# Attention of the first two tiles on diagonal quadrants, with the weight loads cut finer and reordered

## The chip, the cores and the metric

The kernel runs on one core of a Trainium2 chip. The core has a matrix engine, TensorE (PE in the profile; PEld is its loading of weights), a vector engine (DVE), a scalar engine (ACT) for copies and functions such as exp and Gelu, GpSimd (POOL), and SyncE (SP), whose queue issues the DMAs here. SBUF is the working memory, 128 partitions wide; matrix products land in PSUM, which has eight banks of 128 x 512 float32. The metric is the time of one execution on the device, in microseconds.

## What is computed

Attention in chunks of 64 keys, then a two-layer network with an exact Gelu on its result:

```python
q_c = q.reshape(B, H, nc, chunk, D)          # 8, 8, 9, 64, 64; k_c, v_c likewise
scores = scale * np.matmul(q_c, k_c.transpose(0, 1, 2, 4, 3))
attn = softmax(scores)                       # along the last axis
x = np.matmul(attn, v_c)                     # per token the 8 heads side by side: 4608 x 512
h = x @ w_in                                 # 512 x 2048
g = 0.5 * h * (1.0 + erf(h / sqrt(2)))
out = g @ w_out                              # 2048 x 512
```

All inputs and the output are float32; the kernel multiplies in bfloat16.

## The kernel before

The 4608 tokens are handled in nine tiles of 512: tile t takes the first eight chunks of batch t, and the ninth tile the last chunk of every batch. Inside a tile the eight heads form four groups `g` of two; the two heads of a group lie on partitions 0 to 63 and 64 to 127. For each tile there is attention (transposes of q and k, scores, exp, sums, the product with v), which leaves `x` in four parts `x[:, ks, :]`, one for each group; then the first matmul (`h`, 16 blocks `f`, each over the four `ks`, followed by Gelu on ACT) and the second (`y`). From tile 1 on parts of both matmuls are done in seven products instead of eight; from tile 2 on the attention uses four 64x64 quadrants of TensorE (`quad_S`, `quad_av`). All of that stays as it is.

The order of all work is written out by hand (`with tc.manual_schedule()`, L1097): each engine does its instructions in the order in which the lines are run. The change touches the stretch up to tile 1.

**Attention of tiles 0 and 1.** `att_units` makes four lists: `T` (two transposes' units for each group, q then k: `att_Tq`, `att_Tk`), `S_` (`att_S`), `U` (the sums and their reciprocals) and `A` (`att_av`). `att_S` and `att_av` multiply one chunk at a time with a 128x128 block-diagonal left operand, so that both heads of a group go through one full-width matmul of 64 columns. For that, `k_bds` (one for each group) and `v_bds` (one for each tile) hold zeros beside the blocks: `zero_k` on POOL and `zero_v` on DVE for tile 0 (L1105 to L1112), two memsets on POOL for tile 1 (L1172). `att_Tk` copies the transposed k from PSUM in two halves of 64 partitions, `cast_v` casts v in four pieces a group. `transposed` takes its bank from `ps_tp`, which has two; only tile 0's k uses `ps_mm`. The scores and products of tile 1's groups 2 and 3 use `ps_tp` as well, everything else of the attention `ps_at` (three banks, of which one holds y rows during tile 0's second matmul).

**Loads.** All go through SP's queue in the order of the program into six staging buffers (`stage_tile`): tile 0's q and k for each group, v, then w_in in four parts of 1 MB (`load_w_in`; part 0 to 2 as two DMAs each), w_out in four parts (`load_w_out`, one DMA each), with tile 1's q after w_out's first part, its k after the second, and its v last. Each weight part is cast to bfloat16 in four pieces by `win[c](i, ...)` and `wout[c](i, ...)`; piece `i` of `win[c]` is block f = 4c + i, and piece `i` of `wout[c]` is row block f = 4c + i of w_out.

**First matmul of tile 0.** `mm1_slices` (L1203) does f = 0 and 1 with `ks` outermost, `mm1_slot` the others one by one. In tile 0 every 512-column matmul is issued as two of 256 by `by_halves` (its rows stand under L465).

**Second matmul of tile 0.** `phase(0, ..., by_rows=True)` runs 16 steps: step f = 0 to 11 is `mm2_rows(0, f)`, four matmuls for one row block of w_out (L1025; for f = 2 to 4 by halves), and steps 12 to 15 are `mm2_slot` (L989), the last quarter of one of the four token blocks, after which that block is copied out. The dictionary in the call says which units of tile 1's attention stand ahead of which step. TensorE works in this order, so a unit that waits holds up the steps behind it.

```python
        phase(0, {0: [lambda: act_table(Act.Exp)],
                      2: [T[0]], 3: [T[2]], 4: [T[4], T[6]], 7: [T[1], T[3]], 8: [T[5], S_[0]],
                      9: [T[7], S_[1], next_qk], 10: [S_[2], lambda: att_sum(1, 0), lambda: wout[3](2, DV)],
```

Tile 1's first matmul begins right behind (`mm1_slices`, L481), with `A[3]` inside it (`last_av`).

Of the kernel before, what the change touches and what calls it, by code (L numbers as in the profile page):

```python
# [11 lines left out]
def kernel(  # L12
# [10 lines left out]
    P = 128  # L23
# [46 lines left out]

    def zero_v(i, eng):
        eng.memset(v_bds[i][0:CH, :, :, CH:P], 0.0)
        eng.memset(v_bds[i][CH:P, :, :, 0:CH], 0.0)

    def zero_k(k_bd, eng):
        eng.memset(k_bd[0:CH, :, CH:P], 0.0)
        eng.memset(k_bd[CH:P, :, 0:CH], 0.0)
# [99 lines left out]
    def load_v(t):  # L177

        tiles[t]["vf"] = stage_tile()[:].rearrange("p (h n d) -> p h n d", h=H, d=D)
        for h in range(H):  # L180
            nc.sync.dma_start(tiles[t]["vf"][:, h], v[t, h, 0:MT, :].rearrange("(n key) d -> key n d", key=P))  # L181
# [16 lines left out]
    def cast_v(t, g, r, copies):  # L198
        to = slice(CH * r, CH * (r + 1))
        for c, copy in enumerate(copies):  # L200
            copy(v_bds[t % NV][to, c:CT:2, g, to], tiles[t]["vf"][CH * c:CH * (c + 1), 2 * g + r])
# [14 lines left out]
    def att_Tk(t, g, copy):  # L216
        tp = transposed(t, "k", g)
        for r in range(2):
            sl = slice(CH * r, CH * (r + 1))
            copy(k_bds[g][sl, :, sl].rearrange("p i (c j) -> p i c j", j=J), tp[sl])  # L220
# [139 lines left out]

    def att_S(t, g):
# [3 lines left out]
        for i in range(CT):  # L365
            nc.tensor.matmul(s_ps[:, i, :], k_bds[g][:, i, :], st["qT", g][:, i], start=True, stop=True)
# [68 lines left out]
    def att_av(t, g):  # L435
# [3 lines left out]
        for i in range(CT):  # L439
            nc.tensor.matmul(av_ps[:, i, :], v_bds[t % NV][:, i, g, :], st["pT", g][:, i, :], start=True, stop=True)  # L440
# [19 lines left out]
    def by_halves(to, left, right, start, stop):  # L460

        n = to.shape[-1] // 2
        for a in range(2):
            cols = slice(n * a, n * (a + 1))
            nc.tensor.matmul(to[:, cols], left, right[:, cols], start=(start and a == 0), stop=stop, skip_group_check=True)  # L465

    def mm1_slices(t, pools, steps):
# [4 lines left out]
        for step in steps:  # L472
# [3 lines left out]
            for ks in step[1]:  # L476
                for f in step[0]:
# [3 lines left out]
                    (nc.tensor.matmul if t else by_halves)(h_ps[f][:], w_in_sb[:, ks, f * P:(f + 1) * P], st["x"][:, ks, :],  # L481
# [615 lines left out]
    with tc.manual_schedule():  # L1097
# [17 lines left out]
        for g in range(G - 1):  # L1115
            for r in range(2):
                cast_v(0, g, r, (PO, PO))
# [67 lines left out]
        for i in range(FC):  # L1185
            wout[2](i, PO)
# [181 lines left out]
```

## Time and profile before

| | us |
|---|---|
| median of 3 runs | 267.13 (266.97 to 267.51) |
| the profiled execution | 267.09 |
| its span | 265.5 |
| granted TensorE clock, share of full | 0.997 |
| first matmul of tile 0 starts | 17.95 |
| second matmul of tile 0 starts | 32.42 |
| tile 1's first matmul starts | 50.97 |

In the timeline a row holds the start in us, the time to the end of its last instruction, the engine, the line, the operation, what it writes and reads, the shapes, and how many instructions it joins; in brackets stands how long the engine was idle before it and what ended that. A matmul row's end includes the way through the array, so costs of TensorE are better taken from one start to the next. In the chain, each row is the piece of work that the next one waited for. In a table of groups, the numbers behind the first bar are the busy time in us and the mean ns of one, behind the second the idle time before them. In a table of windows, the busy time of each engine is followed by the number of its instructions; the last three columns are the granted clock, the busy share of the 16 DMA engines and GB/s. DMA queue rows give packets, MB and the share of 16 engines' time.

### The profile page before, as it was taken

To read this page: it belongs to the slowest core of one execution; us is meant where nothing else is said; L and a number is where in the kernel's file an instruction comes from. 1 tells how busy PE (TensorE), PEld (TensorE's weight loads), DVE (VectorE), ACT (ScalarE), POOL (GpSimd) and SP (SyncE) were. 2 spreads that over 40 slices of the span, in tenths; PEclk is the share of its full clock that TensorE was granted. 3 is DMA by queue.
4 is the path that set the end of the run, shared out by engine and by line. 5 is a ranking of instruction groups with operands and counts; after the bars stand their busy time and mean duration, and the time that the engine had idled before them with its cause. 6 is when DMAs were issued, how large, how long until landed. Compare 5 with 4: busy or idle time off the path is not lost.

```text
span 265.5 us, 7854 instructions
## 1 busy us (share of the span) xinstructions
PE 256.1 (96%) x3122; PEld 210.6 (79%) x3122; DVE 223.1 (84%) x394; ACT 190.5 (72%) x386; POOL 103.2 (39%) x225
## 2 busy tenths in 40 slices
PE   6789999999999999999999999999999999999993
PEld 2478875556888888887888888888888888888882
DVE  6874986898897599678999999999999999948772
ACT  3856758987767987898888588947894789227720
POOL 7767778702364291481372095009411300000000
PEclk9999999999999999999999999999999999999998
DMA  6999998999979979999999988998973410130014
GB/s 201 268 311 396 395 401 236 283 193 289 243 195 284 220 175 244 275 239 249 276 245 232 267 186 237 217 175 195 264 160 80 134 42 2 41 119 3 2 40 125
DMA packets 123416, 54.02 MB, mean 203 GB/s; under 512 B 97776, under 2 KB 120304, under 8 KB 123376
## 3 DMA queue, kind: packets, MB, share of 16 engines
q1 hardware_dynamic: 123072, 53.23, 77.4%
q8 instruction: 25, 0.41, 0.7%
q10 hardware_dynamic: 304, 0.26, 0.3%
q14 instruction: 15, 0.12, 0.1%
HBM read 36.70 MB, written 9.44 MB: 174 GB/s over the span
## 4 chain that ended last, share of the span: by engine, by line
PE 76%; DMA 10%; ACT 7%; SPq 4%; issue 1%; DVE 0%; POOL 0%
PE hs_ps L601 31%; PE y_ps L761 22%; PE y_ps L791 13%; DMA arrival<-in_moe_w_out_dram 8%; ACT h L609 3%; SPq L181 2%; PE h_ps L491 2%; DMA arrival<-in_moe_w_in_dram 2%; PE av_ps L349 2%; PE h_ps L481 2%; ACT pT L272 2%; SPq L142 1%; PE y_ps L1025 1%; PE y_ps L989 1%; PE s_ps L264 1%; ACT L1095 1%
## 5 line engine op out<-in xcount | busy, mean ns | idle before, releaser
L609 ACT ACTIVATE h<-hs_ps 128x512 bf16<-128x512 f32 x87 | 49.6, 609 | 6.5 <-PE hs_ps L601 5.7
L238 POOL CAST v_nat<-arrival 128x256 bf16<-128x256 f32 x56 | 24.9, 473 | 33.5 <-DMA arrival<-in_v_dram 23.1
L601 PEld LDWEIGHTS <-w_in_sb 128*128 128x128 bf16 x348 | 33.9, 98 | 4.7 <-issue 0.2
L194 POOL CAST q_nat<-arrival 128x256 bf16<-128x256 f32 x40 | 16.8, 467 | 50.2 <-DMA arrival<-in_k_dram 25.3
L601 PE MATMUL hs_ps<-x,w_in_sb 128*128 128x256 bf16 x232 | 31.8, 272 | 0.0
L761 PEld LDWEIGHTS <-h 128*128 128x128 bf16 x240 | 23.2, 98 | 2.8
L1095 ACT ACT_TABLE_LOAD x16 | 20.5, 1283 | 1.3 <-PEq L1352 1.0
L190 POOL CAST k_nat<-arrival 128x256 bf16<-128x256 f32 (+1 forms) x44 | 19.1, 476 | 5.3 <-DMA arrival<-in_k_dram 5.3
L721 ACT COPY kept<-y_ps 128x512 f32<-128x512 f32 (+1 forms) x17 | 9.0, 536 | 16.0 <-PE y_ps L761 15.9
L761 PE MATMUL y_ps<-w_out_sb,h 128*128 128x256 bf16 x160 | 18.6, 273 | 0.0
L761 PE MATMUL y_ps<-v_bd,k_bd 128*128 128x256 bf16 x160 | 18.5, 273 | 0.1
L761 PEld LDWEIGHTS <-k_bd 128*128 128x128 bf16 x160 | 15.6, 98 | 2.1 <-issue 0.2
L618 ACT COPY hs_ps<-hs_ps 128x512 f32<-128x512 f32 x29 | 16.2, 583 | 0.6 <-PE hs_ps L601 0.5
L601 PE MATMUL hs_ps<-k_bd,w_in_sb 128*128 128x256 bf16 x116 | 16.6, 272 | 0.0
L493 ACT ACTIVATE h<-h_ps 128x512 bf16<-128x512 f32 x21 | 12.5, 604 | 5.5 <-PE h_ps L465 4.1
L272 ACT ACTIVATE pT<-s_ps 128x512 bf16<-128x512 f32 x28 | 14.4, 599 | 1.8 <-PE s_ps L264 1.8
L791 PEld LDWEIGHTS <-h 128*128 128x128 bf16 x144 | 13.8, 98 | 1.7
L465 PE MATMUL h_ps<-x,w_in_sb 128*128 128x256 bf16 x128 | 14.5, 273 | 0.1
L601 PE MATMUL hs_ps<-k_bd,w_in_more 128*128 128x256 bf16 x96 | 14.2, 273 | 0.0
L601 PEld LDWEIGHTS <-w_in_more 128*128 128x128 bf16 x128 | 12.5, 98 | 2.0 <-issue 0.3
L726 DVE TENSOR_TENSOR kept<-y_ps,kept 128x512 f32<-128x512 f32 (+1 forms) x16 | 10.4, 651 | 4.3 <-PE y_ps L761 2.3
L465 PEld LDWEIGHTS <-w_in_sb 128*128 128x128 bf16 x128 | 12.3, 98 | 2.1 <-DVE w_in_sb L1070 0.7
(175 smaller groups left out, 638.9 us busy)
## 6 DMA issues: line engine op xcount, KB each, us to landing
arrival<-in_v_dram SPq DMA_DIRECT2D x58, 128.0 KB, 3.2
arrival<-in_k_dram SPq DMA_DIRECT2D x28, 256.0 KB, 5.6
arrival<-in_q_dram SPq DMA_DIRECT2D x7, 1024.0 KB, 6.9
out_dram<-kept SPq DMA_DIRECT2D x24, 256.0 KB, 3.2
arrival<-in_moe_w_out_dram SPq DMA_DIRECT2D x4, 1024.0 KB, 12.1
arrival<-in_moe_w_in_dram SPq DMA_DIRECT2D x6, 512.0 KB, 8.5
out_dram<-y_sb SPq DMA_DIRECT2D x8, 256.0 KB, 2.5
arrival<-in_v_dram SPq DMA_DIRECT2D x28, 64.0 KB, 2.7
```

Source lines behind the costliest of these rows:

```text
L190: copy(st[nm][:, q0:q0 + n, g], st[nm + "f"][:, 2 * q0:2 * (q0 + n), g].rearrange("p (q r) d -> p q r d", r=2))
L194: copy(st[nm][:, g, j:j + 2].rearrange("p j r d -> p r j d"), st[nm + "f"][:, 2 * g:2 * g + 2, j:j + 2])
L238: copy(st["v"][:, r::2, n], st["vf"][:, r::2, n])
L272: nc.scalar.activation(pT[:].rearrange("p u (c j) -> p u c j", j=J), tiles[t]["s_ps"][m // 2][m % 2][:].rearrange("p u (j c) -> p u c j", ...
L465: nc.tensor.matmul(to[:, cols], left, right[:, cols], start=(start and a == 0), stop=stop, skip_group_check=True)
L493: nc.scalar.activation(tiles[t]["h"][:, f, :], h_ps[:], Act.Gelu)
L601: nc.tensor.matmul(hs[:, f], left[:, ks, f * P:(f + 1) * P], right[:, ks], start=(fresh and f == 0 and ks == 0), stop=(ks == 1), skip_grou ...
L609: nc.scalar.activation(h[:, n:n + HM, HD * c:HD * (c + 1)], src, Act.Gelu)
L618: "s11": lambda: AC(place_of("b")[:], bank["a"][:]),
L761: nc.tensor.matmul(to, left(f, m), right[:, f], start=(fresh and (split or m == 0) and f == 0), stop=(f == HF - 1), skip_group_check=True)
L791: nc.tensor.matmul(bank[name][:, m], left(f, m), right[:, f], start=(fresh and m == 0 and f == 0), stop=(f == HF - 1), skip_group_check=True)
L1095: nc.scalar.activation(act_scratch[:], rest[:, 0:1], func)
```

## The change

In tiles 0 and 1, k and v are kept without zeros: the transposed k is copied in one piece into the first 512 columns of `k_bds[g]`, v is loaded so that each head's keys lie on its own 64 partitions and is cast without zeros into the first 2048 columns of `v_bds[t]`. `att_S` and `att_av` do sixteen 64x64 matmuls a group instead of eight full-width ones, alternating between the quadrant of partitions 0 to 63 and that of 64 to 127. All fillings with zeros are gone. w_in's first part comes in four DMAs, every part of w_out and tile 1's q and k in two; w_out's third part is issued ahead of tile 1's k. `by_halves` is gone, and so are the interleaved first two blocks of the first matmul; the order of tile 1's attention among the y rows is new.

```diff
     def load_v(t):
-        tiles[t]["vf"] = stage_tile()[:].rearrange("p (h n d) -> p h n d", h=H, d=D)
+        tiles[t]["vf"] = stage_tile()[:].rearrange("p (g i d) -> p g i d", g=G, d=D)
+        tiles[t]["vr"] = v_bds[t][:].rearrange("p a b c -> p (a b c)")[:, 0:G * MT].rearrange("p (g i d) -> p g i d", g=G, d=D)
         for h in range(H):
-            nc.sync.dma_start(tiles[t]["vf"][:, h], v[t, h, 0:MT, :].rearrange("(n key) d -> key n d", key=P))
+            r = h % 2
+            nc.sync.dma_start(tiles[t]["vf"][CH * r:CH * (r + 1), h // 2],
+                              v[t, h, 0:MT, :].rearrange("(i key) d -> key i d", key=CH))
...
-    def cast_v(t, g, r, copies):
-        to = slice(CH * r, CH * (r + 1))
-        for c, copy in enumerate(copies):
-            copy(v_bds[t % NV][to, c:CT:2, g, to], tiles[t]["vf"][CH * c:CH * (c + 1), 2 * g + r])
+    def cast_v(t, g, copy, n=1):
+        w = CT // n
+        for a in range(0, CT, w):
+            copy(tiles[t]["vr"][:, g, a:a + w], tiles[t]["vf"][:, g, a:a + w])
...
     def att_Tk(t, g, copy):
         tp = transposed(t, "k", g)
-        for r in range(2):
-            sl = slice(CH * r, CH * (r + 1))
-            copy(k_bds[g][sl, :, sl].rearrange("p i (c j) -> p i c j", j=J), tp[sl])
+        kT = k_bds[g][:].rearrange("p i c -> p (i c)")[:, 0:MT].rearrange("p (i c) -> p i c", c=CH)
+        copy(kT.rearrange("p i (c j) -> p i c j", j=J), tp)
+        tiles[t]["kT", g] = kT
...
+    def both_halves(to, left, right):
+        for i in range(CT):
+            for r in range(2):
+                sl = slice(CH * r, CH * (r + 1))
+                nc.tensor.matmul(to(i)[sl], left(i)[sl], right(i)[sl], start=(i == 0), stop=True,
+                                 tile_position=(CH * r, CH * r), skip_group_check=True)
...
-        for i in range(CT):
-            nc.tensor.matmul(s_ps[:, i, :], k_bds[g][:, i, :], st["qT", g][:, i], start=True, stop=True)
+        both_halves(lambda i: s_ps[:, i, :], lambda i: st["kT", g][:, i], lambda i: st["qT", g][:, i])
...
-        for i in range(CT):
-            nc.tensor.matmul(av_ps[:, i, :], v_bds[t % NV][:, i, g, :], st["pT", g][:, i, :], start=True, stop=True)
+        both_halves(lambda i: av_ps[:, i, :], lambda i: st["vr"][:, g, i, :], lambda i: st["pT", g][:, i, :])
...
-                    (nc.tensor.matmul if t else by_halves)(h_ps[f][:], w_in_sb[:, ks, f * P:(f + 1) * P], st["x"][:, ks, :],
+                    nc.tensor.matmul(h_ps[f][:], w_in_sb[:, ks, f * P:(f + 1) * P], st["x"][:, ks, :],
...
-            (by_halves if 2 <= f < 5 else nc.tensor.matmul)(
+            nc.tensor.matmul(
...
     def load_w_out(c):
         raw = stage_tile()[:].rearrange("p (f n) -> p f n", f=FC)
-        nc.sync.dma_start(raw, w_out_v[:, c * FC:(c + 1) * FC, :])
+        for f in range(0, FC, 2):
+            nc.sync.dma_start(raw[:, f:f + 2], w_out_v[:, c * FC + f:c * FC + f + 2, :])
...
-        win = [load_w_in(c, 2) for c in range(NWC - 1)]
+        win = [load_w_in(c, 2 if c else 4) for c in range(NWC - 1)]
...
+        T[2 * G - 2] = lambda: att_Tq(0, G - 1, AC)
...
         for g in range(G - 1):
-            for r in range(2):
-                cast_v(0, g, r, (PO, PO))
-        cast_v(0, G - 1, 0, (PO, PO))
-        win[0](0, PO)
+            cast_v(0, g, PO, 2)
+        win[0](1, PO)
...
-        cast_v(0, G - 1, 1, (DV, DV))
+        cast_v(0, G - 1, DV)
         A[2]()
-        win[0](1, AC)
+        win[0](0, DV)
         p3()
         A[3]()
+        def load_halves(nm):
+            for h in (0, G):
+                load_qk(1, nm, h, h + G)
         win.append(load_w_in(NWC - 1))
         wout = [load_w_out(0)]
-        win[0](2, DV)
+        win[0](2, AC)
         win[0](3, PO)
-        load_qk(1, "q")
+        load_halves("q")
         wout.append(load_w_out(1))
         for c in range(1, NWC):
...
-            if c == 1:
-                load_qk(1, "k")
+            if c == 2:
+                load_halves("k")
             else:
-                wout.append(load_w_out(c))
-            if c < 3:
-                r = slice(CH * (c - 1), CH * c)
-                o = slice(CH * (2 - c), CH * (3 - c))
-                nc.gpsimd.memset(v_bds[1][r, :, :, o], 0.0)
+                wout.append(load_w_out(2 if c == 1 else 3))
...
+        for i in range(FC):
+            wout[2](i, PO if i % 2 == 0 else DV)
         for g in range(G):
             cast_qk(1, "k", g, DV if g % 2 == 0 else PO)
         for i in range(FC):
-            wout[2](i, PO)
-        for i in range(2):
             wout[3](i, PO)
         for g in (0, 2, 3):
-            for r in range(2):
-                cast_v(1, g, r, (PO, PO))
+            cast_v(1, g, PO, 2)
...
-        mm1_slices(0, (mm, mm), (((0, 1), range(KS)),))
         phase(0, {0: [lambda: act_table(Act.Exp)],
-                      2: [T[0]], 3: [T[2]], 4: [T[4], T[6]], 7: [T[1], T[3]], 8: [T[5], S_[0]],
-                      9: [T[7], S_[1], next_qk], 10: [S_[2], lambda: att_sum(1, 0), lambda: wout[3](2, DV)],
-                      11: [lambda: wout[3](3, AC), S_[3]], 12: [lambda: cast_v(1, 1, 0, (AC, AC)), lambda: cast_v(1, 1, 1, (AC, AC)), sums],
-                      13: [A[0], lambda: over[0](2), lambda: over[0](3), U[1]], 14: [A[1], U[2]], 15: [A[2], U[3]]},
-              by_rows=True, first=2)
+                      4: [T[0], T[2], T[4]], 5: [T[6]], 9: [next_qk], 11: [T[1], T[3]],
+                      12: [T[5], T[7], S_[0], S_[1], S_[2], lambda: att_sum(1, 0), S_[3], lambda: cast_v(1, 1, AC)],
+                      13: [sums], 14: [A[0], lambda: over[0](2), lambda: over[0](3), U[1]], 15: [A[1], U[2]],
+                      "end": [A[2], U[3]]},
+              by_rows=True)
```

18 lines of the change are left out of this document (1 added, 17 removed).

## The prediction

> **What bounds the kernel now.** I read the page first, then the chain that ended last, then the timeline of TensorE (PE) and of its weight loads (PEld) from 17 to 51 us, where the change acts.
>
> ```profile
> span 265.5 us, 7854 instructions
> PE 256.1 (96%) x3122; PEld 210.6 (79%) x3122; DVE 223.1 (84%) x394; ACT 190.5 (72%) x386; POOL 103.2 (39%) x225
> PE 76%; DMA 10%; ACT 7%; SPq 4%; issue 1%; DVE 0%; POOL 0%
> ...
> 11.87 5.30 DMA arrival<-in_moe_w_in_dram
> ...
> 18.78 22.29 DMA arrival<-in_moe_w_out_dram x2
> 41.13 0.62 POOL w_out_sb L1078
> 41.79 1.02 PE y_ps L1025 x4
> ```
>
> Three quarters of the chain is PE. The DMA share lies wholly before 41 us: first w_in, then w_out. So two things count: when the first FFN starts and is fed, and how densely PE runs from there to tile 1, which starts at 50.97. After that the chain is PE again, and I carry a shift there to the end one to one.
>
> ```profile
> 17.63 0.41 PE L440 MATMUL av_ps<-pT,v_bd 128*128 128x64 bf16 x8
> 18.36 0.69 DVE L442 TENSOR_TENSOR x<-av_ps,rc 128x512 bf16<-128x512 f32 x1 [0.89 <-ACT rc L431]
> 21.17 0.43 DVE L1070 CAST w_in_sb<-arrival 128x512 bf16<-128x512 f32 x1 [1.74 <-DMA arrival<-in_moe_w_in_dram]
> 17.95 3.39 PEld L465 LDWEIGHTS <-w_in_sb 128*128 128x128 bf16 x32
> 21.65 3.39 PEld L465 LDWEIGHTS <-w_in_sb 128*128 128x128 bf16 x32 [0.31 <-DVE w_in_sb L1070]
> 25.42 6.88 PEld L465 LDWEIGHTS <-w_in_sb 128*128 128x128 bf16 x64 [0.38 <-DVE w_in_sb L1070]
> 34.37 1.04 PE L465 MATMUL y_ps<-w_out_sb,h 128*128 128x256 bf16 x8
> 37.66 1.89 PE L1025 MATMUL y_ps<-w_out_sb,h 128*128 128x512 bf16 x8
> 39.38 0.61 PE L207 MATMUL tp<-ident,k_nat 128*128 128x128 bf16 x8
> 39.83 1.03 PE L1025 MATMUL y_ps<-w_out_sb,h 128*128 128x512 bf16 x4
> ```
>
> An f of the first FFN is eight half matmuls. f=4 waits for w_in's second part: it lands at 21.17, is cast, and PE goes on at 21.65. f=8 waits again, at 25.42. So **the first FFN runs at the heels of w_in's DMA**, not of its own start at 17.95. From start to start, eight 512-wide matmuls take 39.38 - 37.66 = 1.72, so 0.86 for four, and two transposes of a pair 39.83 - 39.38 = 0.45, 0.22 each.
>
> ```profile
> 32.42 1.89 PE L1025 MATMUL y_ps<-w_out_sb,h 128*128 128x512 bf16 x8
> 41.03 0.38 PE L207 MATMUL tp<-ident,k_nat 128*128 128x128 bf16 x4 [0.17 <-ACT k_bd L220]
> 41.25 0.40 PE L366 MATMUL s_ps<-s_sb,k_bd 128*128 128x64 bf16 x8
> 43.97 0.40 PE L366 MATMUL s_ps<-s_sb,k_bd 128*128 128x64 bf16 x8
> 44.20 0.38 PE L374 MATMUL sum_ps<-pT,ones_bd 128*128 128x512 bf16 x1
> 45.52 1.03 PE L1025 MATMUL y_ps<-w_out_sb,h 128*128 128x512 bf16 x4
> 46.48 0.40 PE L392 MATMUL sums_ps<-pT,ones_c 128*32 128x512 bf16 x4
> 46.81 1.04 PE L989 MATMUL y_ps<-w_out_sb,h 128*128 128x512 bf16 x4
> 50.97 0.59 PE L481 MATMUL h_ps<-x,w_in_sb 128*128 128x512 bf16 x2
> ```
>
> From 32.42 to 50.97 (18.55) PE does the second matmul of tile 0 with tile 1's attention strewn between. It loses only 41.03 - 39.83 - 0.86 = 0.34 (a transpose waits for a bank), 41.79 - 41.25 - 0.23 = 0.31 (w_out's third part, by the chain) and 46.48 - 45.52 - 0.86 = 0.10: 0.75 in all. A score group of eight costs 44.20 - 43.97 = 0.23.
>
> **The change, part by part.**
>
> *Fillings and casts.* Gone are the memsets and more than half of the v casts; the k copies are halved.
>
> ```profile
> L1172 POOL MEMSET v_bd<- 64x2048 bf16 x2 | 3.6, 1797 | 0.1
> L201 POOL CAST v_bd<-arrival 64x256 bf16<-64x256 f32 x26 | 10.4, 399 | 1.4
> L238 POOL CAST v_nat<-arrival 128x256 bf16<-128x256 f32 x56 | 24.9, 473 | 33.5 <-DMA arrival<-in_v_dram 23.1
> L220 ACT COPY k_bd<-tp 64x512 bf16<-64x512 bf16 x12 | 6.9, 578 | 5.9 <-PE tp L207 5.8
> 23.74 2.37 DVE L1070 CAST w_in_sb<-arrival 128x512 bf16<-128x512 f32 x2 [0.87 <-DMA arrival<-in_moe_w_in_dram]
> ```
>
> In tile 0, 14 POOL casts of 0.399 become 6 of about 0.473 (5.6 to 2.8 us), and each k copy is one of 0.58 instead of two. That takes about 1 us from the road to x[3], now ready at 18.36 + 0.69 = 19.05. It buys nothing by itself, since f=4 is tied to the DMA. It also counts once that two DVE casts took 2.37 from 23.74 while a POOL memset ran, against 0.43 for one at 21.17: without memsets the wait at 25.42 goes, 25.42 - 21.65 - 4 x 0.87 = 0.29.
>
> *w_in's first part in four.* The contiguous rows go from 256 to 128 float32, 1 KB to 512 B.
>
> ```profile
> 12.00:13.00 1.00, 0.43 (x10) 0.32 (x9) 0.97 (x3) 0.96 (x3) 0.88 (x3) 1.00 0.94 212
> 22.00:23.00 1.00, 1.00 (x12) 0.90 (x10) 0.43 (x1) 0.52 (x2) 0.59 (x2) 1.00 1.08 393
> ```
>
> With 256 B rows (v, first window) the DMA engines, equally busy, moved 212 GB/s; with mostly 1 KB rows (second) 393. 512 B is not in the trace. Bounds for this 1.05 MB: 2.67 us at 393, 4.95 at 212, so 0 to 2.3 us more. By time per row (16 engines: 19 ns and 42 ns), a third of the way is 27 ns, 306 GB/s, 3.4 us: I take **+0.7 us** for everything behind it, f=4 first. The Trainium skill, DMA: Bandwidth & Descriptors, Specifications, puts the smallest transfer at line rate at 512 B; by that this term is nearer 0 and the sum 0.7 us lower. The trace has no row for it.
>
> So f=4 at 21.65 + 0.7 = 22.35, then twelve f of 0.86 without the wait: 32.7 against 32.42, **+0.3**. The plain matmuls for `by_halves` give only 0.87 - 0.86 = 0.01 an f.
>
> *Issue order.* Six DMAs of w_out and tile 1's q and k become twelve, two of w_in four; SP runs 5 to 13 us ahead of the landings (the first w_in part: issued 11.87, landed 5.30 later), which hides their 0.5 us each; uncovered, 2 us or more. w_out's third part, landing about 41.1 now, comes about 2.6 us earlier (a 1 MB slot at 400 GB/s), so the 0.31 goes, and k lands where it did. PE would want k for T1 at about 43.7: hidden by 2 us.
>
> *The hand-written order of tile 1.* Here PE is in order, and I price the new lumps. T0, T2, T4 now stand together, with two banks in `ps_tp`.
>
> ```profile
> 34.15 0.39 PE L207 MATMUL tp<-ident,q_nat 128*128 128x128 bf16 x4
> 34.64 0.57 ACT L213 COPY s_sb<-tp 128x512 bf16<-128x512 bf16 x1
> 44.41 0.60 ACT L368 ACTIVATE pT<-s_ps 128x512 bf16<-128x512 f32 x1 [0.50 <-PE s_ps L366]
> 45.72 0.60 ACT L368 ACTIVATE pT<-s_ps 128x512 bf16<-128x512 f32 x1 [0.21 <-PE s_ps L366]
> ```
>
> T4 must wait until T0's copy frees its bank: 34.64 + 0.57 - 34.15 = 1.06 after T0's start, but PE is there after 0.44: **+0.62**, with f=4's matmuls queued behind. At step 12 stand T5, T7, S0 to S2, the sum, S3. From the end of f=11 at 0: T5's copy ends at 1.06 by the same rows, and the first exp, whose scores would let it start 0.44 after them (43.97 to 44.41), stands behind that copy on ACT and ends at 1.66. The sum starts 0.16 later, at 1.82 (as 45.72 + 0.60 to 46.48 now), S3 at 2.04. The four exps follow one another on ACT to 1.06 + 4 x 0.60 = 3.46, so `sums` can't start before 3.62, though S3 and the 0.86 of y work after it are done by 3.2. It ends 0.33 later (46.81 - 46.48), at 3.95. The same work without waits costs 0.44 + 4 x 0.23 + 0.22 + 0.86 + 0.33 = 2.77: **+1.18**. Behind these waits stand S3, the y rows and A0, for which tile 1 waits.
>
> *Diagonal quadrants.* A group of eight becomes sixteen on 64x64.
>
> ```profile
> 93.28 0.67 PE s_ps L264 x64
> 101.59 0.64 PE av_ps L349 x64
> ```
>
> Later tiles run 64 of them on all four quadrants in 0.67. From one side a quarter of that, 0.17; from the other sixteen in sequence at 0.23 / 8, 0.47. I take 0.32, near the middle and by the nearest row: the 128x32 sums took 46.81 - 46.48 = 0.33 for what four column groups side by side could do in 0.22, so a small tile among full-width work costs about 0.1 beyond its own time. That is +0.09 for each of A0 to A3, **+0.36** (bounds -0.24 and +0.96). The score groups hide under the exp waits above. A rule that speaks against the change: the Trainium skill, TensorEngine Tiling (Array Packing), Key Properties, says that a change of tiling mode drains TensorE; by it each of these groups pays at both ends, and if it didn't hold here the sum would be 0.4 lower. The 0.33 agrees with it.
>
> **Sum.** +0.3, +0.62, +1.18, +0.36, less the 0.75 of waits now: **+1.7 us**. The profiled execution took 267.09 (span 265.5 and 1.6 around it); the median of the runs is 267.13. So 268.8.
>
> **Rivals.**
>
> *Faster: the start is freed.* The second w_in part lands before PE wants it. For it: the first part took 5.30 us from issue to landing, though 0.52 MB needs 1.3 at 393 GB/s, so its feed is not bound by the rate alone; and an instruction fetch took about 1 us of one DMA engine just before the second part landed:
>
> ```profile
> q8 instruction: 1, 0.02, 6.0%
> ```
>
> (6.0% of 16 engines in the window 19 to 20, so 0.96 us of one). If the fetch falls elsewhere, f=0 ends at about 17.95 + 0.22 with the earlier x[3], and fifteen f follow: 31.07, -1.35. With quadrants at 0.17 the rest is 0.62 + 1.18 - 0.24 - 0.75 = +0.81. Together -0.54: 266.5. Against it: new PE instructions in front (8 groups of 16) pull the fetch forward, not away.
>
> *No change.* The start gains its 1.35, but quadrants cost 0.32, and the lumps give it all back (0.62 + 1.18 + 0.36 - 0.75 = +1.41): 267.2. What speaks for it is that both sums come from the same rows; against it, that they would have to cancel.
>
> *Slower still: the feed falls behind.* A second instruction fetch comes before f=4, as there are more PE instructions in front of it: 0.96 us more, f=4 at 23.3, the first FFN's end at 33.6, +1.2, with the +1.41 behind it: 269.7. Against it: the fetch need not fall on the DMA engine that lands last.
>
> **How the numbers follow.** Forecast 268.8, chance 0.44, by itself 267.7 to 269.6. Freed start 0.32, no change 0.12, slower still 0.12. Less than 0.2% (0.53 us) can't be told from no change here. So faster 0.32, same 0.12, slower 0.56; the range, 266.0 to 269.8, takes in the freed start and the slower feed.
>
> **What would show it.** Right: f=4's weight loads after 22; 0.6 us idle ahead of the third q transpose; `sums` waiting for the last exp; av groups over 0.23; tile 1's first matmul near 52.7. Wrong: f=4 without a DMA wait before 21.2, the first FFN over by 31.3, or quadrant groups of 0.2; and a tile 1 that starts later without the end moving would break the one-to-one step.

## The result, and the profile after

The changed kernel takes 270.78 us in the median of 5 runs (269.0 to 272.82); the kernel before, beside it on the same chip, 267.51 (266.97 to 270.08): 1.013 times the time (1.0085 to 1.0177). Its profiled execution took 269.0 with a span of 267.4, the shortest of the five, 1.9 above the profiled 267.09 of before. So there are two questions: what the 1.9 are, and why the usual execution takes nearly two more.

The page and the chain of waits to 60 us (as in the prediction, the first FFN is tile 0's first matmul, the second FFN its second):

```profile
span 267.4 us, 7927 instructions
PE 257.7 (96%) x3174; PEld 204.3 (76%) x3174; DVE 215.5 (81%) x389; ACT 186.3 (70%) x377; POOL 90.7 (34%) x201
PE 83%; ACT 7%; SPq 5%; DMA 2%; issue 1%; DVE 0%
...
11.47 0.63 SPq L175
12.15 0.62 SPq L1061
...
15.49 5.94 DMA arrival<-in_moe_w_in_dram
21.94 10.53 PE h_ps L485 x48
```

w_out has left the chain; w_in's arrival is still in it, and ahead of it stand SP's issues of v (L175), as they did in the kernel before (L181). TensorE's timeline, from the first FFN to tile 1:

```profile
17.61 3.73 PE L485 MATMUL h_ps<-x,w_in_sb 128*128 128x512 bf16 x16 [0.28 <-DVE w_in_sb L1064]
21.94 10.53 PE L485 MATMUL h_ps<-x,w_in_sb 128*128 128x512 bf16 x48 [0.60 <-DVE w_in_sb L1064]
32.31 3.62 PE L1019 MATMUL y_ps<-w_out_sb,h 128*128 128x512 bf16 x16
35.76 0.61 PE L202 MATMUL tp<-ident,q_nat 128*128 128x128 bf16 x8
36.82 0.38 PE L202 MATMUL tp<-ident,q_nat 128*128 128x128 bf16 x4 [0.45 <-ACT s_sb L208]
...
44.62 0.61 PE L202 MATMUL tp<-ident,k_nat 128*128 128x128 bf16 x8
45.16 0.96 PE L361 MATMUL s_ps<-s_sb,k_bd 64*64 64x64 bf16 x48
46.29 0.38 PE L376 MATMUL sum_ps<-pT,ones_bd 128*128 128x512 bf16 x1 [0.17 <-ACT pT L370]
46.59 0.44 PE L361 MATMUL s_ps<-s_sb,k_bd 64*64 64x64 bf16 x16
46.97 1.04 PE L983 MATMUL y_ps<-w_out_sb,h 128*128 128x512 bf16 x4
47.93 0.40 PE L394 MATMUL sums_ps<-pT,ones_c 128*32 128x512 bf16 x4
48.26 1.04 PE L983 MATMUL y_ps<-w_out_sb,h 128*128 128x512 bf16 x4
49.23 0.44 PE L361 MATMUL av_ps<-pT,v_bd 64*64 64x64 bf16 x16
49.60 1.04 PE L983 MATMUL y_ps<-w_out_sb,h 128*128 128x512 bf16 x4
...
52.28 0.82 PE L475 MATMUL h_ps<-x,w_in_sb 128*128 128x512 bf16 x3
```

and the four exps of step 12 on ACT:

```profile
45.64 2.06 ACT L370 ACTIVATE pT<-s_ps 128x512 bf16<-128x512 f32 x4
```

Read from start to start:

- The second FFN starts at 32.31, 0.11 earlier than before.
- The third q transpose starts 36.82 - 35.76 = 1.06 after the first of its lump; two transposes without a wait take 0.44. **+0.62.**
- Step 12 takes 47.93 - 44.62 = 3.31 from its first transpose to `sums`, where the same work without waits takes 2.44 (the prediction's 2.77 less the 0.33 of `sums`). **+0.87.** The only wait named in it is 0.17 ahead of the sum.
- A product group takes 49.60 - 49.23 = 0.37 where it took 0.23, and stands 49.23 - 48.26 = 0.97 behind four y matmuls that took 0.87 (46.81 to 47.68): **+0.24** a group, 0.72 for A0 to A2.
- Of the old 0.75, the waits of 0.34 and 0.31 are gone. The 0.10 ahead of `sums` is not (47.93 - 46.97 = 0.96, as 46.48 - 45.52 before); it lies within the 3.31, so taking off the whole 0.75 counts it once.

0.62 + 0.87 + 0.72 - 0.75 = 1.46; from the second FFN's start to tile 1 it is 52.28 - 32.31 = 19.97 against 18.55, 1.42 more. A3 adds its 0.24. The later tiles' first rows show a shift of 1.56 that stays (69.64 to 71.20, 236.77 to 238.33), and the span's end adds 0.3, which is not followed up here. So the profiled execution is understood but for that. The other executions are not, by this.

### The profile page after: what moved, and what is told of

It is laid out like the page before. It is cut to its first block, busy times and chain, and to the rows that moved or that the text cites. A ratio compares the mean times of both kernels' runs of the same rounds, so it can differ in the third digit from the quotient of the medians.

```text
span 267.4 us, 7927 instructions
## 1 busy us (share of the span) xinstructions
PE 257.7 (96%) x3174; PEld 204.3 (76%) x3174; DVE 215.5 (81%) x389; ACT 186.3 (70%) x377; POOL 90.7 (34%) x201
## 4 chain that ended last, share of the span: by engine, by line
PE 83%; ACT 7%; SPq 5%; DMA 2%; issue 1%; DVE 0%
PE hs_ps L595 30%; PE y_ps L755 22%; PE y_ps L785 13%; PE h_ps L485 6%; PE y_ps L1019 4%; ACT h L603 3%; SPq L175 3%; DMA arrival<-in_moe_w_in_dram 2%; PE h_ps L475 2%; PE av_ps L344 2%; ACT pT L267 2%; PE y_ps L983 1%; SPq L134 1%; PE s_ps L259 1%; SPq L1061 1%; ACT L1090 1%
## 5 line engine op out<-in xcount | busy, mean ns | idle before, releaser
L233 POOL CAST v_nat<-arrival 128x256 bf16<-128x256 f32 x56 | 26.1, 493 | 33.7 <-DMA arrival<-in_v_dram 31.4
L595 PEld LDWEIGHTS <-w_in_sb 128*128 128x128 bf16 x348 | 33.9, 98 | 4.7 <-issue 0.2
L189 POOL CAST q_nat<-arrival 128x256 bf16<-128x256 f32 x40 | 15.7, 444 | 50.1 <-DMA arrival<-in_k_dram 28.0
L485 PE MATMUL h_ps<-x,w_in_sb 128*128 128x512 bf16 x92 | 21.1, 379 | 0.9 <-DVE w_in_sb L1064 0.9
L487 ACT ACTIVATE h<-h_ps 128x512 bf16<-128x512 f32 x23 | 13.7, 603 | 6.2 <-PE h_ps L485 6.2
L485 PEld LDWEIGHTS <-w_in_sb 128*128 128x128 bf16 x92 | 8.8, 98 | 11.1 <-DVE w_in_sb L1064 1.5
```

The source lines that it names most:

```text
L189: copy(st[nm][:, g, j:j + 2].rearrange("p j r d -> p r j d"), st[nm + "f"][:, 2 * g:2 * g + 2, j:j + 2])
L233: copy(st["v"][:, r::2, n], st["vf"][:, r::2, n])
L485: nc.tensor.matmul(h_ps[:], w_in_sb[:, ks, f * P:(f + 1) * P], tiles[t]["x"][:, ks, :], start=(ks == 0), stop=(ks == KS - 1))
L487: nc.scalar.activation(tiles[t]["h"][:, f, :], h_ps[:], Act.Gelu)
L595: nc.tensor.matmul(hs[:, f], left[:, ks, f * P:(f + 1) * P], right[:, ks], start=(fresh and f == 0 and ks == 0), stop=(ks == 1), skip_grou ...
```

## The experiments

All share one scheme, and a table of two marks carries most of it: F, the start of the second FFN in the profiled execution, and T, the start of tile 1's first matmul. The median is over all runs of the kernel, the ratio is to the kernel before, run beside it on the same chip (medians of 266.6 to 266.9, and 267.51 for the line of the changed kernel). The ratio is not the quotient of the two medians, and the two can differ: for again the medians are 3.8 us apart, and the ratio of 1.0097 is 2.6 us. Differences in us below are of medians, and the intervals reach 0.5 to 1.3 us to either side. In before_quads one of F's matmuls is missing in the trace, so its F may be 0.2 too late.

| kernel | F | T - F | T | median | ratio (interval) |
|---|---|---|---|---|---|
| before | 32.42 | 18.55 | 50.97 | 267.13 | 1 |
| changed | 32.31 | 19.97 | 52.28 | 270.78 | 1.0131 (1.0085 to 1.0177) |
| again | 33.47 | 19.97 | 53.44 | 270.36 | 1.0097 (1.0057 to 1.0137) |
| win_two | 33.13 | 19.97 | 53.10 | 269.93 | 1.0105 (1.0070 to 1.0139) |
| order_spread | 32.44 | 20.32 | 52.76 | 269.68 | 1.0105 (1.0071 to 1.0139) |
| before_quads | 33.30 | 20.45 | 53.75 | 270.43 | 1.0117 (1.0078 to 1.0157) |
| vhalf_alone | 33.80 | 18.25 | 52.05 | 268.61 | 1.0064 (1.0032 to 1.0096) |
| quads_vfull | 31.99 | 19.60 | 51.59 | 268.67 | 1.0067 (1.0037 to 1.0098) |
| pe_more | 32.26 | 18.25 | 50.51 | 267.46 | 1.0012 (0.9980 to 1.0044) |
| before_lumps | 34.19 | 24.05 | 58.24 | 273.72 | 1.0241 (1.0193 to 1.0289) |
| before_lumps2 | 32.37 | 20.54 | 52.91 | 269.88 | 1.0115 (1.0084 to 1.0146) |
| after_vfull | 33.64 | 19.97 | 53.61 | 269.65 | 1.0108 (1.0082 to 1.0133) |
| after_full | 34.19 | 19.99 | 54.18 | 271.23 | 1.0159 (1.0129 to 1.0190) |
| after_full_spread | 34.14 | 18.22 | 52.36 | 268.41 | 1.0060 (1.0031 to 1.0090) |
| full_dv | 32.49 | 19.99 | 52.48 | 269.62 | 1.0099 (1.0068 to 1.0131) |
| full_spread_dv | 31.89 | 18.50 | 50.39 | 268.18 | 1.0054 (1.0031 to 1.0077) |
| before_win_four | 33.47 | 18.25 | 51.72 | 266.88 | 1.0004 (0.9978 to 1.0029) |
| after_vfull_spread | 33.75 | 20.35 | 54.10 | 269.55 | 1.0084 (1.0054 to 1.0114) |
| k_first | 31.58 | 18.22 | 49.80 | 267.69 | 1.0041 (1.0022 to 1.0060) |
| k_first_early | 32.32 | 18.22 | 50.54 | 267.85 | 1.0037 (1.0015 to 1.0059) |

Theories at the outset, with the letters of the expectations: the recorded steps are the whole of it (M); the usual execution loses its time in w_in's feed (there F, not the mark), late in the kernel (L), through the time of instruction fetches (I), through the quadrants or v's load to halves of the partitions (Q, V), or in the lumps of the new order.

**again: the changed kernel, unaltered**

> The changed kernel unaltered. Its profiled execution took 269.0 (tile 1's first matmul at 52.28, +1.3 against before), but four other executions took 270.3 to 272.8. Theory M (the recorded steps are the whole of it): on one chip its median stands 1.5 to 2.0 us over the kernel before, and the spread is in both kernels. Theory F (the feed): slow executions are those in which w_in lands late; if this profile is one of over 270, f=4's weight loads stand after 22.5 and everything behind is shifted by as much. Theory L (later): tile 1 starts at 52.3 again and a slow execution loses its time behind 72 us.

270.36. The chain of its profiled execution (270.9, span 269.4):

```profile
14.50 1.48 SPq L1061
17.12 7.21 DMA arrival<-in_moe_w_in_dram
24.83 5.78 PE h_ps L485 x26
```

T - F is 19.97 to the digit; F is 1.16 later than in the first profile. So the stretch behind F is fixed, and the time in front of F varies. A second loss lies later: the shift against the kernel before is 2.77 at 129 us and 3.42 at 206. This profiled execution is the longest of the seven. The clock is not the reason: the seven have a mean granted clock of 0.997 to 1.0.

**win_two: w_in's first part in two**

```diff
-        win = [load_w_in(c, 2 if c else 4) for c in range(NWC - 1)]
+        win = [load_w_in(c, 2) for c in range(NWC - 1)]
```

> The changed kernel with w_in's first part in two DMAs, as before, instead of four. M: the 512 B rows cost 0.7, so f=4's weight loads come at 21.2 to 21.5 instead of 21.94, and the end 0.4 to 0.7 us earlier. F: the same, and the spread gets smaller, so that the median falls by 1 us or more. Rival (finer parts help): f=0 starts 0.5 later, at 18.1, and nothing is gained.

269.93, not told apart from the changed kernel.

**before_win_four: the same question from the other side** (the kernel before, with the first part in four)

> The kernel before with w_in's first part loaded in four transfers of 128 columns, nothing else. The recorded sum has +0.3 at the first FFN's end: 267.1, with the first wait for w_in_sb in the FFN. If 512 B rows cost nothing, within 0.2 of the kernel before. If the finer rows are what makes the usual execution late, +1 or more.

Ratio 1.0004 (0.9978 to 1.0029): the four transfers cost nothing that can be told from noise, and at most 0.8 us. (F is late in its profile because the clock halved; see after_full.)

**pe_more: instruction fetches moved** (the kernel before, 71 short matmuls in place of seven long ones at the start)

```diff
-        keep_warm(7)
+        warm = ps_mm.tile([P, MT], f32, tag="mm", name="warm")
+        for _ in range(71):
+            nc.tensor.matmul(warm[:, 0:48], rest[:, 0:P], rest[:, 0:48], start=True, stop=True)
```

> The kernel before with 64 more pairs of weight load and matmul at its very start (71 warming matmuls of 48 columns for 7 of 512, about the same time), nothing else. I: the first instruction fetch moves from 19 to about 14 us and the second from 27 to about 21, f=4's weight loads come 0.5 to 1 us later, the end +0.5 to +1.5 us. V and Q: no change, within 0.3 us.

The fetches moved from 19.03 and 27.01 to 9.94 and 21.18 us, F stayed, and 1.0012 (0.9980 to 1.0044) isn't told from no change; a loss of more than 1.2 us is excluded. So by this test their time doesn't make a loss of 3 us.

**before_quads: quadrants and v's new load on the kernel before** (the diff's `load_v`, `cast_v`, `att_Tk`, `both_halves`, `att_S`, `att_av`, no zeros)

> The kernel before with the diagonal quadrants alone (k and v dense, no zeros, v loaded by halves of partitions, fewer casts and copies); DMAs, halves and order as before. M: each of tile 1's eight groups costs 0.1 more, the third q-k bank wait shrinks, f=8 no longer waits for DVE: between -0.2 and +0.8 us, most likely +0.4. Rival (quadrants are the loss): +1.5 us or more. Rival (they are a gain): -0.5 or less, by the POOL work gone.

270.43, +3.8: as much as the whole change, without its order and its other transfers. Of its T - F of 20.45, 0.64 is a late k: the first k transpose starts at 40.96, 38.60 + 1.72 = 40.32 would have been its time.

**vhalf_alone: only v's load to 64 partitions**, cast from there into the same zero-filled tile

```diff
-            nc.sync.dma_start(tiles[t]["vf"][:, h], v[t, h, 0:MT, :].rearrange("(n key) d -> key n d", key=P))
+            r = h % 2
+            nc.sync.dma_start(tiles[t]["vf"][CH * r:CH * (r + 1), h // 2],
+                              v[t, h, 0:MT, :].rearrange("(i key) d -> key i d", key=CH))
```

> The kernel before with one thing changed: each head's v goes by DMA to 64 partitions instead of 128; zeros, full-width matmuls, casts in four pieces, all order as before. Theory V (the v load is the hidden loss: with it tile 0's v landed at 16.1 and later instead of 14.2, and all weights behind it): v's last landing after 15.5, f=4's weight loads after 22.3, the end 1.5 to 3 us later. Theory Q (the quadrants alone lose): no change, within 0.4 us. Theory I (earlier PE instruction fetches hit the feed): no change either, since PE's instructions are the same.

268.61, +1.7, and T - F is 0.30 shorter, since the old wait of 0.31 for w_out is gone: all of the loss lies in front of F. The view of one line's instructions (duration in ns least, median, most; first and last start), before and here:

```profile
L181 SPq DMA_DIRECT2D arrival<-in_v_dram x8: 468/514/1882, 5.1 to 11.3; - x8
```

```profile
L182 SPq DMA_DIRECT2D arrival<-in_v_dram x8: 633/747/1702, 5.1 to 12.6; - x8
```

and SP's timeline, before and here:

```profile
5.06 6.76 SPq L181 DMA_DIRECT2D arrival<-in_v_dram x8
11.87 5.49 SPq L1067 DMA_DIRECT2D arrival<-in_moe_w_in_dram x6
```

```profile
5.08 8.13 SPq L182 DMA_DIRECT2D arrival<-in_v_dram x8
13.25 5.98 SPq L1069 DMA_DIRECT2D arrival<-in_moe_w_in_dram x6
```

No issue to 64 partitions is under 0.63 us, and the eight last until w_in's first issue, 13.25 - 11.87 = **1.38 late; F is 33.80 - 32.42 = 1.38 late.** The DMA engines aren't the brake, they idle more:

```profile
12.00:13.00 1.00, 0.72 (x14) 0.60 (x14) 1.00 (x2) 0.28 (x1) 0.94 (x4) 1.00 0.76 174
13.00:14.00 1.00, 0.40 (x8) 0.10 (x5) 0.96 (x3) 0.96 (x3) 0.94 (x3) 1.00 0.87 198
14.00:15.00 1.00, 0.81 (x13) 0.42 (x13) 0.87 (x3) 1.00 (x2) 0.94 (x4) 1.00 0.80 169
```

174, 198 and 169 GB/s with engines 0.76 to 0.87 busy; the kernel before moved 212 in the first of these windows at 0.94. The Trainium skill, DMA: Bandwidth & Descriptors, Rules for kernel authors, advises against two transfers to disjoint halves of the partitions: they share the same engines, and one transfer to 128 partitions is to be used. The advice agrees with these rows. The reason that it names is not what they show: the price is in the issue, with the engines less busy.

The same reading holds over all profiles. F comes 19.9 to 20.7 us after w_in's first issue in 13 of the 16 profiles whose clock stayed full (before 32.42 - 11.87 = 20.55; changed 32.31 - 12.15 = 20.16; again 33.47 - 13.28 = 20.19; k_first 31.58 - 11.13 = 20.45); the others are pe_more (19.8), after_vfull_spread (21.2) and after_vfull (21.4). The eight v issues take 5.7 to 7.2 us in the 14 profiles with v on 128 partitions, 6.3 to 7.8 in the 6 with 64; the medians are 6.4 and 7.35, **0.95 apart**, though the ranges overlap: order_spread has 64 partitions and issued w_in at 11.75.

**quads_vfull: only the quadrants** (v loaded and cast in pieces as before)

> The kernel before with the diagonal quadrants, but v loaded to 128 partitions and cast in four pieces, as before. V: of the 3.8 us that quadrants with the new v load cost, 1.5 to 3 come back, and what is left is +1.0 to +1.5 (0.14 for each of eight groups in front of tile 1's first matmul, measured at 0.37 against 0.23). Q: still +3 or more. I: f=4 after 22.2 and +2 to +3, with the first two 16 KB instruction fetches near 13 and 22 us instead of 19 and 27.

268.67, +1.8, and now F is early and T - F is 1.05 longer. TensorE's timeline:

```profile
40.26 0.39 PE L200 MATMUL tp<-ident,k_nat 128*128 128x128 bf16 x4
40.58 0.44 PE L359 MATMUL s_ps<-s_sb,k_bd 64*64 64x64 bf16 x16
40.95 1.04 PE L1024 MATMUL y_ps<-w_out_sb,h 128*128 128x512 bf16 x4
...
46.70 1.04 PE L988 MATMUL y_ps<-w_out_sb,h 128*128 128x512 bf16 x4
47.67 0.44 PE L359 MATMUL av_ps<-pT,v_bd 64*64 64x64 bf16 x16
48.04 1.04 PE L988 MATMUL y_ps<-w_out_sb,h 128*128 128x512 bf16 x4
```

A group lasts 0.37 (40.58 to 40.95), for scores and products alike, and starts 0.10 later behind its predecessor (40.26 to 40.58 is 0.32, a full-width group there starts after 0.22). So 0.24 more than the 0.23 before; seven groups lie between F and T, 1.68, less two old waits (0.34 and 0.31) that are gone: 1.03, measured 1.05.

**order_spread: the changed kernel with its transposes and score groups one or two to a step**

```diff
-                      4: [T[0], T[2], T[4]], 5: [T[6]], 9: [next_qk], 11: [T[1], T[3]],
-                      12: [T[5], T[7], S_[0], S_[1], S_[2], lambda: att_sum(1, 0), S_[3], lambda: cast_v(1, 1, AC)],
+                      2: [T[0]], 3: [T[2]], 4: [T[4], T[6]], 8: [T[1], T[3]], 9: [T[5], S_[0], next_qk],
+                      10: [T[7], S_[1]], 11: [S_[2], lambda: att_sum(1, 0)], 12: [S_[3], lambda: cast_v(1, 1, AC)],
```

> The changed kernel with tile 1's transposes and scores strewn between the y rows one or two at a time (q at steps 2 to 4, k from 8 on, scores 9 to 12); sums and products stay at 13 to end. M: the wait of the third q transpose (0.45 idle) and those around the sum go: 0.9 to 1.3 us faster than the changed kernel. F: the lumps matter little, 0.3 or less. Rival: k lands too late for step 8 and the waits come back there, 0 to 0.4 us.

269.68, hardly less; T - F even rises to 20.32. k is cast late (its transpose waits at 40.73; behind four row blocks from 36.78 on, 36.78 + 4 x 0.86 = 40.22 would have been its time), and each score group stands alone and pays its 0.24, of which the lump had saved a part.

**before_lumps and before_lumps2: the new order alone on the kernel before** (the diff's steps; the second casts w_out's last part on POOL alone)

> The kernel before with the order alone: f=0 and 1 one after the other, and tile 1's units at steps 4, 5, 11, 12, 13 to end as in the changed kernel. M (the recorded terms): +0.62 and +1.18 less the 0.75 of waits that it has now: tile 1's first matmul 0.9 to 1.2 us later, the end as much. Rival (PE would have waited for weights anyway): within 0.3 us.

> The kernel before with the new order of tile 1's steps alone, w_out's last part now cast by POOL alone, so that no cast stands between the steps (that is what spoilt the first try, +6.5). By the recorded sum the order costs 0.62 at step 4 and 1.18 at step 12, less 0.3 to 0.75 of waits that go: +1.0 to +1.5. If the lumps are worth little, within 0.4 of the kernel before; if w_out's casts are late again, far above, and then the wait in front of w_out's matmuls shows it.

The first, 273.72, says nothing on the order: w_out's last casts, put behind step 12, held its matmuls up by 1.48 and 0.71, and the clock was halved ahead of F and again behind these waits, from 53 to 57 us (mean 0.985). The second: 269.88, +3.0, twice what was expected. T - F is 20.54, of which 0.36 is a wait for w_out.

**after_vfull and after_vfull_spread: the changed kernel, v loaded as before; and with the spread order**

> The changed kernel with one thing taken back: v of the first two tiles is loaded to all 128 partitions and cast in pieces as before; the quadrants, the other transfers and the order stay. If the load of v to 64 partitions costs what it cost alone (+1.7), this is 1.3 to 2.0 us under the changed kernel, about 268.4 to 268.9 where the kernel before has 266.8, and v's last part lands near 14.5 us, not 16 or 17; the first FFN starts earlier by about as much. If the load's cost was only that of being added to the kernel before, and is hidden behind the changed kernel's later w_in parts, it equals the changed kernel (270 to 270.8).

> The changed kernel with v loaded and cast as before and the steps of tile 1 spread. If the lumps are worth 1.4 also with the quadrants, it is 1.4 under the version with v alone put back (269.65): near 268.2, with 18.9 to 19.2 us from the second FFN's first matmul to tile 1's (19.97 with the lumps). If k lands late again, near 40 us, the wait takes the gain and it stays at 269 to 270.

269.65 and 269.55. Against 270.36 to 270.78 the first may gain 0.7 to 1.1, but the intervals overlap, and its F (33.64) is no earlier: w_in was issued at 12.23, yet F came 21.4 later, which stays unexplained. The second shows again that this spread order buys nothing with quadrants (20.35), and again k's transpose waits (0.37 named, at 42.08). With quadrants and the order of the kernel before T - F is 19.60 (quads_vfull).

**after_full and after_full_spread: the changed kernel with full-width matmuls, zeros and v as before; and spread**

> What is left of the change without its quadrants: the transfers of w_in, w_out, q and k in their new pieces and order, the new order of the steps of tile 1, copies not by halves; the matmuls are full-width over zeros and v is loaded and cast as before. The groups of scores and of products are 0.23 again. If the quadrants and the load of v make the whole loss (1.8 + 1.7 in 3.8), this lands within 0.5 of the kernel before, or up to 0.5 faster: 266.2 to 267.2. If the lumps at the second FFN's steps 4 and 12 cost the 1.8 that the recorded sum gives them, it is 267.8 to 268.6.

> The same, with the q and k transposes and the score groups of tile 1 one or two to a step (steps 2, 3, 4, 8, 9, 10, 11, 12) in place of the lumps at steps 4 and 12. If lumps cost as the recorded sum has it (0.62 + 1.18), it is 1 to 1.8 us under the version with the lumps, and 0.5 to 1.5 faster than the kernel before. If k's landing sets the steps (it landed at 40 us in the earlier run with such an order), it is no faster than the version with the lumps.

271.23 and 268.41, both far from what was expected, since F is 1.7 late in each. The windows of after_full:

```profile
13.00:14.00 1.00, 0.10 (x3) 0.10 (x4) 0.93 (x3) 0.96 (x3) 0.90 (x3) 1.00 0.98 246
...
15.00:16.00 1.00, 0.99 (x20) 0.99 (x20) 0.47 (x3) 1.00 (x1) 0.87 (x3) 0.52 1.15 344
16.00:17.00 1.00, 1.00 (x12) 0.92 (x11) 1.00 (x2) 0.46 (x2) 0.84 (x3) 0.50 1.07 257
17.00:18.00 1.00, 1.00 (x11) 0.67 (x9) 0.94 (x3) 0.00 (x0) 0.94 (x2) 0.50 0.97 272
18.00:19.00 1.00, 1.00 (x18) 0.92 (x18) 0.45 (x2) 0.59 (x1) 0.38 (x2) 0.77 1.03 325
```

TensorE stood idle for 1.05 us ahead of 13.90, waiting for a k copy that stood behind the last q copy on ScalarE; then the granted clock fell to 0.52, 0.50, 0.50, 0.77. The missing shares add up to 1.71 us. The changed kernel has that line too (`T[2 * G - 2]`, next test), but its k copy is a single one.

**full_dv and full_spread_dv: the same without that line**

```diff
-        T[2 * G - 2] = lambda: att_Tq(0, G - 1, AC)
```

> The version with full-width matmuls and the whole new order, without the line that moves tile 0's last transposed q to ScalarE. That line kept a k copy waiting 1.05 us at 12.8 to 13.9 and the granted clock then fell to 0.50 to 0.52 for 3 us (the products' sums took 1.98 where they take 1.09). If the clock made the 1.8 by which the first FFN ended late, this is 1.5 to 2 us under the earlier try: 269.2 to 269.8, with a first FFN that ends near 32.4 and 19.9 to 20.1 us from there to tile 1's first matmul (18.55 in the kernel before). If the lumps cost nothing in time, it is 266.5 to 267.2.

> The same with the spread order. If both the clock and the lumps are what cost the time, nothing is left of the loss: 266.0 to 267.0 against 266.8 of the kernel before, FFN end near 32.2 and 18.2 from there to tile 1's first matmul. The difference to the version with the lumps prices them: 1.4 to 1.8 by the recorded sum. If the finer transfers of w_in delay the first FFN by themselves, it is 0.3 to 1.0 over the kernel before, with w_in_sb named ahead of the FFN's matmuls.

F falls by 34.19 - 32.49 = 1.70, and the clock stays at 1.00: in the profiled execution the clock was the cause. For the median it isn't shown: three of after_full's six executions have a mean clock of 0.998 to 1.0 and still took 269.7 to 271.5. Nor is it shown that the wait of 1.05 halved the clock: before_win_four and before_lumps, without that line, fell as low, and win_two (a wait of 1.08) and before_quads (1.16) kept 1.00. **The lumps alone cost 269.62 - 268.18 = 1.44** (T - F 19.99 against 18.50, 1.49), side by side on one chip, with full-width matmuls. But full_spread_dv, whose profile is level with the kernel before (span 265.5 both), is 1.0054 in the median.

**k_first and k_first_early: k ahead of w_out's third part again, which POOL alone casts, behind k; and the steps of the kernel before**

```diff
-            if c == 2:
+            if c == 1:
                 load_halves("k")
             else:
-                wout.append(load_w_out(2 if c == 1 else 3))
+                wout.append(load_w_out(c))
```

> The version with full-width matmuls, last q on VectorE and spread order, with the second k loaded and cast ahead of w_out's third part again, as in the kernel before. In its earlier form (268.18) k landed at 39.5 us with the fifth of its transposes at 40: any late execution then waits for it. If k's place makes the 1.4 us by which its usual execution is longer than its profiled one (267.01), it is 266.2 to 267.0, level with the kernel before or up to 0.5 faster. If the w_in feed or the halved clock makes them, it stays at 267.7 to 268.5.

> The same, with tile 1's k transposes, score groups, sums and products at the steps of the kernel before (7, 8, 9, 10, 11, 12, 13, 14, 15), so that the products are one row block earlier and the wait of 0.24 for VectorE ahead of tile 1's third matmul goes. What is left of the change is then the pieces of the transfers and the matmuls of the first FFN that are not cut in halves. If nothing else of the change costs time, 266.0 to 266.8 against 266.7 of the kernel before; 0.2 to 0.5 under the other of this call.

267.69 and 267.85: k's place is worth little, and a part of the loss is still there. The profile of k_first says where. Tile 1 starts at 49.80, **1.17 earlier than in the kernel before**; at 118 us 0.71 of that is left, and then:

```profile
126.64 1.91 PE L784 MATMUL y_ps<-v_bd,s_sb 128*128 128x256 bf16 x16
129.18 0.71 PE L264 MATMUL s_ps<-q_t,k_t 64*64 64x64 bf16 x64 [0.63 <-DMA k_t<-k_nat]
```

The kernel before, same rows:

```profile
127.42 1.91 PE L791 MATMUL y_ps<-v_bd,s_sb 128*128 128x256 bf16 x16
129.26 0.71 PE L264 MATMUL s_ps<-q_t,k_t 64*64 64x64 bf16 x64
```

A transposed k of a later tile lands when it lands; the lead of 0.78 becomes a wait of 0.63. From there to 206 us k_first loses 0.69 more (129.18 to 206.99 against 129.26 to 206.38) without a wait named on TensorE; from 140 to 180 us VectorE is busy 9.7 to 9.9 of every 10 us in both kernels. No version beat the kernel before.

## Why the prediction was wrong, step by step

**The direction, and most of the mechanism from F to T, were right.** The prediction made that stretch 52.7 - 32.7 = 20.0; it is 19.97 in four profiles. The q lump is exact (1.06 from first to third transpose, +0.62). Step 12 was mis-sized at +1.18: it is +0.87. The prediction let the four exps follow one another at 4 x 0.60 = 2.40; they take 2.06, since each starts 0.48 to 0.49 behind the one before it: 0.34 less, about the whole difference of 0.31. `sums` was said to wait for the last of them. No wait shows: it stands 0.96 behind the y row, as in the kernel before, and the last exp, at 45.64 + 2.06 = 47.70, is done 0.23 ahead of it. So the score groups hide no more than in part: the exps would have held `sums` to about the same time, but what fills the 0.87 in the trace is the wait of 0.17 and the small matmuls with their edges. With full-width groups and two copies to each k it is 48.81 - 44.80 - 2.44 = 1.57 (full_dv). w_out's third part gave its 0.31 back. T fell at 52.28, and the shift passes to the end one to one in the profiled execution.

**The quadrant term was mis-sized.** "I take 0.32, near the middle and by the nearest row" gave +0.09 a group and +0.36. A group takes 0.37 and starts 0.10 late: +0.24, +0.96 for the four. That this is the upper bound to the digit is chance, for the bound priced sixteen matmuls one after another. The row taken, 128x32 sums of 0.33, priced one edge only. That two errors of -0.31 and +0.60 in one sum partly cancel is luck.

**The step that failed is the issue order.** It said that SP "runs 5 to 13 us ahead of the landings [...], which hides their 0.5 us each", counted w_out, q, k and w_in, and left out v, so that its load to 64 partitions stood at nothing in the sum, though its eight issues stand right before w_in's in the same queue. To 64 partitions each takes at least 0.62 to 0.63 in place of 0.47 to 0.51, SP has no lead at that point, and w_in's first issue moves with them: 0.93 later in the median of the profiles, 1.38 in the test of it alone, and F with it. That test costs 1.7 us (1.0064). In the changed kernel itself the step is not confirmed: with v's load put back (after_vfull) the time falls by no more than the noise. The chain of the kernel before held the clue, in the rows ahead of the one that the prediction starts with:

```profile
6.14 1.11 SPq L181
7.29 1.88 SPq L181
9.22 0.96 SPq L181
11.87 5.30 DMA arrival<-in_moe_w_in_dram
```

SP's issues of v (L181) stood on the chain, with w_in's first issue directly behind them.

**The feed term (+0.3) priced something else.** It priced 512 B rows; four transfers in place of two can't be told from nothing (1.0004), and +0.3 lies within that interval. That w_in sets F was right, and so was "the first FFN runs at the heels of w_in's DMA". "Freed start" is in no profile of the changed kernel. Something near it is seen in k_first, with full-width matmuls and the earliest w_in (issued at 11.13): its first FFN runs from 17.95 to 31.58 without a wait, 0.84 ahead of the kernel before, and even so the kernel is not faster. "Slower still" had the right place and about the right size (F at 33.6; again 33.47), but its cause, instruction fetches, moved 9 us in pe_more without a loss that can be told from noise.

**The one profile was taken for the usual execution.** The changed kernel's first profile had the second shortest v issues among the six with 64 partitions (w_in's first issue at 12.15, in again at 13.28) and was the shortest of its five runs. With 0.93 more in front of F, 1.42 to T and 0.24 for A3, the usual execution is 2.6 over the kernel before; measured are 3.3 and 3.8 by the medians, 3.5 and 2.6 by the ratios. So between nothing and 1.2 us is not accounted for. A part appears in again, the longest of its seven executions, behind 129 us (0.65), where k_first loses too. What makes it is open: that a later k holds TensorE up by 0.63 and that VectorE is nearly always busy is seen in k_first; that they are the cause of the rest is argued only.

**The parts don't add.** Quadrants with v's load alone cost 3.8, the order alone 3.0, the whole change 3.3 to 3.8. Part of it is in T - F: 20.45 with one (0.64 of it a late k), 20.54 with the other (0.36 of it a wait for w_out), 19.97 with both. The clearest pair has one order: 19.97 with quadrants (after_vfull), 19.99 with full-width matmuls (full_dv). What the quadrants cost there, the single k copies give back: full_dv's lump waits 0.17, 0.15 and 0.26 for k copies that are double, the changed kernel's for none. So undoing one of the two (after_vfull, order_spread) hardly showed. For the time in front of F, which differs too, this is not worked out.

## What to carry to other kernels

When a load's shape changes, price its issue on the queue too, and ask which load is issued next: eight issues 0.12 us longer each moved the one load that feeds TensorE by a microsecond. A small-tile group among full-width work pays at both edges; price it from a row that stands alone, not from a packed one. And take parts off singly only beside a test with both off: two changes that share a wait can look free when one of them is undone.

## What was not expected of the hardware

- A 128 KB load to 64 partitions took SP at least 0.62 to 0.63 us to issue, to 128 partitions 0.47 to 0.51, with the DMA engines less busy (0.76 to 0.87 from 12 to 15 us in vhalf_alone against 0.94 from 12 to 13 in the kernel before).
- Sixteen 64x64 matmuls between full-width ones cost 0.47 (0.10 ahead, 0.37 for themselves), where 64 of them together cost 0.67 in the later tiles. Two such groups in a row take 0.62 in the changed kernel (13.86 to 14.48), so by estimate 0.25 of the 0.37 are the matmuls and 0.12 the edge behind them.
- In four profiles (after_full, after_full_spread, before_win_four, before_lumps) the granted clock fell to 0.50 for about 3.4 us from 15 us on (before_win_four: 0.64, 0.50, 0.50, 0.66 from 15 to 19) and cost 1.7 us. From 5 us on no wait of TensorE ahead of it is longer than 1.35 us (before_lumps, up to 7.72). A wait of about 1 us is not enough by itself: win_two (1.08 us), again (1.00 us) and before_quads (1.16 us) kept the full clock. What decides it stays open. The Trainium skill, TensorE: Matmul & The Clock Gate, Part 1, describes a free-running window of about 3.4 us after which an idle array runs at half speed; the half speed and its length agree with these windows, but no idle stretch of that length stands in them.
